# RWKV-6 with mixture-of-depths: another written order of the turns, and the shift issued by SP

## The chip, the cores and the metric

One core of a Trainium2 chip runs the whole kernel. The metric is the device time of one execution in microseconds (us). The kernel before took 281.06 us (median of three runs, 280.52 to 287.19); a further execution was profiled.

## The reference, cut to what matters

Inputs: r, k, v, w of shape (4 samples, 8 heads, 768 steps, 48), u (8, 48), and a router with two weight matrices.

```
for t in range(768):                     # per sample and head, state is 48 x 48
    y[t]  = r[t] @ (state + outer(u * k[t], v[t]))
    state = w[t][:, None] * state + outer(k[t], v[t])
x = y with heads side by side            # (4, 768, 384)
scores = x @ w_gate
for each sample: for the 128 rows with the highest score:
    out[row] = x[row] + sigmoid(score) * (relu(x[row] @ w1) @ w2)
all other rows: out[row] = x[row]
```

## The kernel before, in words

**Tiles.** A sample's 768 steps are cut into 6 chunks of 128, so there are 24 chunks, n = 0 to 23. A chunk of an input is a tile of 128 steps x 384 (8 heads x 48), 192 KB. Inside a chunk the recurrence is written as matmuls. The decay is taken in logarithms: `lnw` (ACT, line 136) takes ln w; `sums` (line 140) sums them along the steps with a triangular matmul (PE, L145) and ACT makes `fall` (L148) and `rise` (L159), the exponentials of the sum and of its negative. `e` is `fall` moved up by one step. For the first three chunks it is a second matmul and exponential (L154, L155); from then on it is the **shift**: two DMAs from SBUF to SBUF, one of 112 rows and one of 15, issued by ACT (L158). `line` (L165) writes one row of `fall` to DRAM, `whole` (L173) reads it back across the partitions as `all`, the chunk's whole decay.

`scaled` (DVE, L204) makes K = k * e and R = r * rise. `turned` (L215, L217) transposes both with eight PE transposes and copies them out of PSUM on ACT as Kt and Rt. `scores` (L235) multiplies them in quarters into a PSUM buffer P, of which there are two, used in turn (`p_bufs[n % 2]`); `fresh` (L251) puts the new state's products in the same buffer; `masked` (DVE, L263) makes `sc`; `states` makes s1 and mid (DVE, L276 to L281) and the next chunk's state s0 (POOL, L283). `from_state` (L294) and `from_chunk` (L312) add the two parts of the result into P. `own_products` (POOL, L180, L181), `own_sum` (DVE, L188) and `own_values` (POOL, L195) make the part with u. `result` (DVE, L334, L340) adds it to P, giving x, takes the router's score, and SP stores x (L344).

**The order is written by hand.** One loop runs over turns, n = -4 to 23. A turn does different stages of different chunks: `sums` of chunk n+4, `scaled` of n+3, `turned` of n+2, `scores` and `states` of n+1, the result of n. Every engine works through its own instructions in the written order, and so does the queue of SP, which issues all loads, stores, `line` and `whole`. At a turn's end `load` fetches w, k, r and v of chunk n+7. Each of the first seven turns also loads a piece of w1 or w2 (L537; three of 512 KB, four of 384 KB).

**The mixture.** When a sample's six chunks are done, `mixture` finds its 128 best rows and runs the two matmuls. It is a generator of 28 pieces, which the next sample's six turns take up, 4 or 5 a turn, half of them in the middle of the turn and the rest at its end: two `every` (PE L356, ACT L359), six `ahead` (DVE, L369), the rank (PE L378), pick, index and gather (DVE L393, PE L399, POOL L412), `xeT` (L420, L422), the gate, eight pieces of `ps_h` (L451, with `hid` on ACT, L456, after each four), and eight of `ps_f` (L461), the last with `ye` (DVE, L467) and a scatter (POOL, L470). All share one PSUM buffer, so `ps_e` of the second half waits until `every` of the first has been copied, and so on. The last sample's mixture runs alone at the end.

**A wait put in by hand.** `from_state` and `from_chunk` write other rows of the same PSUM bank, so `from_chunk` waits on an instruction of ACT that comes after `from_state`: the copy of Kt of the same turn (`after`, L219). Where none is named, ACT copies two columns of P first (`seen`, L308).

Of the kernel before, what the change touches and what calls it, by code (L numbers as in the profile page):

```python
# [17 lines left out]
L = 128  # L18
# [5 lines left out]
def _rows(ap, n):  # L24

    return dataclasses.replace(ap, ap=[[0, n]] + [list(x) for x in ap.ap])
# [10 lines left out]
def kernel(  # L37
# [14 lines left out]
    nc = tc.nc  # L52
# [6 lines left out]
    NCH = S // L  # L59
# [19 lines left out]
    chunks = [(b, ci) for b in range(B) for ci in range(NCH)]  # L79
# [14 lines left out]
    all_bufs = [consts.tile([L, HP], FP32, name=f"all_buf{i}") for i in range(6)]  # L94

    work = {n: {} for n in range(N)}

    def load(n, names="wkrv"):
        if n >= N:
            return  # L100
        b, ci = chunks[n]
        for name in names:
            x, bufs = dict(w=(w, 5), k=(k, 7), r=(r, 7), v=(v, 10))[name]
            t = lev.tile([L, H, D], FP32, tag=name, name=name, bufs=bufs)
            src = x[b, :, ci * L:(ci + 1) * L, :].rearrange("h t d -> t h d")
            nc.sync.dma_start(out=t, in_=src)  # L106
            work[n][name] = t
# [22 lines left out]


    def lnw(n):
        if n < N:
            t = work[n]
            t["lw"] = lev.tile([L, C], FP32, tag="lw", name="lw", bufs=2)
            nc.scalar.activation(  # L136
                out=t["lw"], in_=t.pop("w").rearrange("p h d -> p (h d)"), func=AF.Ln
            )

    def sums(n):  # L140
        if not 0 <= n < N:
            return
        t = work[n]
        ps = psR.tile([L, 512], FP32, tag="r", name="ps_x")
        nc.tensor.matmul(ps[:, 0:C], tri, t["lw"], start=True, stop=True)  # L145
        fall = t["fall"] = lev.tile([L, C], FP32, tag="fall", name="fall")
        rise = t["rise"] = lev.tile([L, C], FP32, tag="rise", name="rise")
        nc.scalar.activation(  # L148
            out=fall, in_=ps[:, 0:C], func=AF.Exp, accum_out=guard[:, n, 0:1]
        )  # L150
        e = t["e"] = e_bufs[n % len(e_bufs)]
        if n < EARLY:
            strict = psR.tile([L, 512], FP32, tag="r", name="ps_x")
            nc.tensor.matmul(strict[:, 0:C], tri_s, t["lw"], start=True, stop=True)  # L154
            nc.scalar.activation(out=e, in_=strict[:, 0:C], func=AF.Exp)  # L155
        else:
            for lo, hi in ((0, L - 16), (L - 16, L - 1)):
                nc.scalar.dma_start(out=e[lo:hi], in_=fall[lo + 1:hi + 1])  # L158
        nc.scalar.activation(  # L159
            out=rise, in_=ps[:, 0:C], func=AF.Exp, scale=-1.0, accum_out=guard[:, n, 1:2]  # L160
        )

    def line(n):
        if 0 <= n < N:
            nc.sync.dma_start(out=lines[n:n + 1], in_=work[n]["fall"][0:1])  # L165
# [24 lines left out]
    def own_values(n):  # L190
        if not 0 <= n < N:
            return
        t = work[n]
        t["vo"] = lev.tile([L, H, D], FP32, tag="vo", name="vo")
        nc.gpsimd.tensor_mul(t["vo"], t["v"], t.pop("own").to_broadcast([L, H, D]))  # L195
# [12 lines left out]
    def turned(n):  # L208
        if not 0 <= n < N:
            return  # L210
        t = work[n]
        for name in "KR":
            ps = psR.tile([L, HP, L], FP32, tag="r", name="ps_t")
            for j in range(HP):
                nc.tensor.transpose(ps[:, j, :], t[name][:, 2 * j:2 * j + 2, :], ident)  # L215
            t[name + "t"] = lev.tile([L, HP, L], FP32, tag=name + "t", name=name + "t", bufs=3)
            ins = nc.scalar.copy(out=t[name + "t"], in_=ps)  # L217
            if name == "K":
                after[n - 2] = ins  # L219
        t.pop("R")  # L220

    after = {}
    quarters = [(par, sub) for par in (0, 1) for sub in (0, 1)]

    def half(i, n=HB):
# [101 lines left out]
    def result(n):  # L327
        if not 0 <= n < N:
            return
        t = work.pop(n)  # L330
        b, ci = chunks[n]
        x = lev.tile([L, C], FP32, tag="x", name="x", bufs=3)
        pairs = dict(q=2, d=D)
        nc.vector.tensor_add(  # L334
            x.rearrange("p (j q d) -> p q j d", **pairs),
            t["P"][:, :, 0:YW].rearrange("p q (j d) -> p q j d", d=D),
            t["vo"].rearrange("p (j q) d -> p q j d", q=2),
        )
        scr = lev.tile([L, C], FP32, tag="scr", name="scr")
        nc.vector.tensor_tensor_reduce(  # L340
            out=scr, in0=x, in1=wg_bc, scale=1.0, scalar=0.0, op0=ALU.mult, op1=ALU.add,
            accum_out=score[:, b, ci:ci + 1],
        )
        nc.sync.dma_start(out=views[b][b, ci * L:(ci + 1) * L, :], in_=x)  # L344
# [132 lines left out]
    def run(*steps):  # L477
        for g in steps:
            yield from g
# [3 lines left out]
    def mix(n):  # L483
        for _ in range(n):
            next(mixing, None)
# [4 lines left out]
    with tc.manual_schedule():  # L490
        nc.scalar.preload_act_table_set("natural_log_exp_and_others")
        load(0, "wkr")
        load(1, "wkr")
        nc.sync.dma_start(out=u_bc, in_=_rows(u, L))
        load(0, "v")
        load(1, "v")
        load(2)
        nc.sync.dma_start(out=wg_bc, in_=_rows(moe_w_gate, L))
        load(3)

        nc.gpsimd.iota(row, pattern=[[1, L]], base=0, channel_multiplier=0)
        nc.gpsimd.iota(col, pattern=[[0, L]], base=0, channel_multiplier=1)
        nc.vector.tensor_tensor(out=tri, in0=col, in1=row, op=ALU.is_ge)
        for t in e_bufs:
            nc.gpsimd.memset(t[L - 32:L], 1.0)
        nc.vector.tensor_tensor(out=tri_s, in0=col, in1=row, op=ALU.is_gt)
        nc.vector.tensor_tensor(out=ident, in0=col, in1=row, op=ALU.is_equal)
        for t in k_bufs + r_bufs:
            nc.vector.memset(t[:, :, D:HB], 0.0)
        for t in all_bufs:  # L510
            nc.gpsimd.memset(t, 1.0)
        nc.vector.tensor_tensor(out=behind[:, 0:L], in0=col, in1=row, op=ALU.is_lt)
        for i in (0, 1):
            nc.vector.tensor_copy(out=mask[half(i)], in_=behind[half(i), half(i)])
            nc.vector.memset(p_bufs[i], 0.0)
        nc.vector.tensor_copy(out=slots, in_=row)
        nc.vector.memset(ones, 1.0)
        nc.vector.memset(ones_f, 1.0)
        nc.gpsimd.memset(behind[:, L:S], 1.0)
        nc.gpsimd.iota(count, pattern=[[-L, NCH]], base=S - 1, channel_multiplier=-1)  # L520
        nc.vector.tensor_copy(out=behind_n, in_=count)
        nc.gpsimd.iota(
            number[:, :, :, 0], pattern=[[S, B], [L, NCH]], base=0, channel_multiplier=0
        )
        nc.gpsimd.iota(
            number[:, :, :, 1], pattern=[[0, B], [0, NCH]], base=0, channel_multiplier=1
        )
        nc.vector.tensor_copy(out=ids, in_=number)

        lnw(0)  # L530
        for n in range(-4, N):
            if n >= 0 and chunks[n][1] == 0 and n > 0:
                mixing = run(mixing, mixture(chunks[n][0] - 1))
            k1 = per_turn[chunks[n][1]] if n >= NCH else 0
            if n >= 0 and n < len(weights):
                to, of = weights[n]
                nc.sync.dma_start(out=to, in_=of)  # L537
            whole(n + 3)
            lnw(n + 5)
            from_state(n)  # L540
            turned(n + 2)
            scores(n + 1)
            fresh(n + 1)
            own_values(n + 1)
            masked(n + 1)
            states(n + 1)
            mix(k1 // 2)
            from_chunk(n)
            result(n) if n >= 0 else None
            own_products(n + 3)  # L550
            own_sum(n + 2)
            sums(n + 4)
            line(n + 4)
            load(n + AHEAD)
            scaled(n + 3)
            mix(k1 - k1 // 2)
        mixing = run(mixing, mixture(B - 1))
        mix(1000)

        total = setup.tile([L, 1], FP32)  # L560
        nc.vector.tensor_reduce(out=total, in_=guard, axis=AX.XY, op=ALU.add)
        ps = psM.tile([L, C], FP32, tag="m", name="ps_w")
        nc.tensor.matmul(ps[0:1, 0:1], total, ones_f, start=True, stop=True)
        wide = setup.tile([1, 1], INT32)
        nc.vector.tensor_scalar(
            out=wide, in0=ps[0:1, 0:1], scalar1=LIMIT, scalar2=0.5, op0=ALU.is_le, op1=ALU.is_lt
        )
# [72 lines left out]
```

## Time and profile before

| what | before |
|---|---|
| median of three runs | 281.06 us (280.52 to 287.19) |
| the profiled execution | 279.03 us |
| its span, first to last instruction | 277.2 us |
| mean TensorE clock granted | 0.821 |
| PE matmul, weight load | 201.8 us (73%), 153.6 us (55%) |
| DVE, ACT, POOL busy | 141.2 (51%), 76.9 (28%), 96.8 us (35%) |
| DMA moved | 34.29 MB |
| 31 to 90 us: PE busy, clock, DMA | 48.80 us, 0.71, 185 GB/s |
| 90 to 224 us: PE busy, clock, DMA | 107.63 us, 0.89, 123 GB/s |
| 224 to 277 us: PE busy, clock, DMA | 30.95 us, 0.81, 25 GB/s |
| `masked` of chunks 0, 1, 8, 13, 23 begins | 28.1, 33.55, 90.56, 137.1, 227.9 us |

A profile line of a group names the code line, the engine, the operation and output<-inputs. PEld is the load of a matmul's fixed operand; SPq and ACTq are the sequencers that issue DMAs. In a line of the timeline, the brackets at the end hold how long the engine had been idle and what ended it. In the chain that ended last, each piece was released by the one before it, or by its engine's previous instruction. The clock is a share of full speed; it was 0.50 or 1.00 in every stretch of the trace.

### The profile page before, as it was taken

The numbers are of one execution on the slowest core, as the hardware profiler recorded it, in microseconds if no ns is written. First come the engines' busy times: TensorE is split into PE (matmuls) and PEld (weight loads), VectorE is DVE, ScalarE is ACT, GpSimd is POOL, SyncE is SP. The second block draws the span as 40 slices with busy tenths as digits, with TensorE's granted clock in tenths as the row PEclk, the third lists the DMA queues.
The fourth block names the chain that finished last, engine by engine and source line by source line (L and its number), as shares of the span: only waits on it lengthen the run. The fifth ranks groups of instructions, "written<-read, shape, count | busy, mean of one in ns | idle before, by whom it ended". The sixth has DMA issues, their size and how long they took to land.

```text
span 277.2 us, 8475 instructions
## 1 busy us (share of the span) xinstructions
PE 201.8 (73%) x3592; PEld 153.6 (55%) x3592; DVE 141.2 (51%) x330; ACT 76.9 (28%) x198; POOL 96.8 (35%) x119
## 2 busy tenths in 40 slices
PE   3336769877987568999875889998749799527750
PEld 1115556756665357766554767676538675317620
DVE  7210657551567938535689376346893641451010
ACT  3316333232333234233442241425312101100100
POOL 5400555046232565432554255235443410110010
PEclk9955975775579659999987699999876999955995
DMA  7899795879886878677776544672211000100010
GB/s 150 181 202 203 146 220 118 211 161 202 205 205 174 195 171 181 131 161 172 172 160 135 114 112 101 137 170 87 61 58 31 31 31 31 57 16 15 0 35 8
DMA packets 121508, 34.29 MB, mean 124 GB/s; under 512 B 113651, under 2 KB 120694, under 8 KB 121462
## 3 DMA queue, kind: packets, MB, share of 16 engines
q1 hardware_dynamic: 117632, 28.00, 47.0%
q10 hardware_dynamic: 3318, 4.10, 5.1%
q0 software_dynamic: 512, 1.57, 1.8%
q8 instruction: 30, 0.49, 0.8%
q14 instruction: 16, 0.13, 0.1%
HBM read 24.02 MB, written 5.54 MB: 107 GB/s over the span
## 4 chain that ended last, share of the span: by engine, by line
PE 35%; DVE 21%; issue 15%; DMA 12%; SPq 9%; ACT 4%; POOL 1%; ACTq 1%; DVEq 0%; POOLq 0%
PE ps_t L215 6%; SPq L106 6%; PE ps_h L451 6%; DMA w<-in_w_dram 5%; PE ps_p L312 5%; PE ps_p L235 4%; PE ps_f L461 4%; DVE r_buf L204 4%; DVE ahead L369 3%; PE ps_x L145 3%; DVE k_buf L204 3%; PE ps_p L251 3%; DVE x L334 2%; DMA e_buf<-fall 2%; DVE sc L263 2%
## 5 line engine op out<-in xcount | busy, mean ns | idle before, releaser
L263 DVE TENSOR_TENSOR sc<-ps_p,mask 128x512 f32<-128x512 f32 x24 | 16.6, 691 | 61.1 <-PE ps_p L251 61.1
L283 POOL TENSOR_TENSOR s<-mid,all_buf 128x192 f32<-128x192 f32 x20 | 11.7, 586 | 91.2 <-DVE mid L281 39.7
L312 PE MATMUL ps_p<-v,sc 64*64 64x48 f32 x768 | 32.2, 242 | 6.2 <-ACT Kt L217 6.2
L312 PEld LDWEIGHTS ps_p<-v,sc 64*64 64x64 f32 x768 | 29.3, 157 | 11.4 <-ACT Kt L217 6.8
L195 POOL TENSOR_TENSOR vo<-v,own 128x384 f32<-128x384 f32 x24 | 23.4, 974 | 21.7 <-DVE own L188 21.5
L451 PE MATMUL ps_h<-xeT,w 128*128 128x128 f32 x192 | 27.8, 299 | 3.4 <-ACT hid L456 2.8
L145 PE MATMUL ps_x<-lw,tri 128*128 128x384 f32 x48 | 27.0, 651 | 4.3 <-ACT lw L136 4.3
L334 DVE TENSOR_TENSOR x<-ps_p,vo 128x384 f32<-128x384 f32 x24 | 13.3, 556 | 31.8 <-PE ps_p L312 26.3
L451 PEld LDWEIGHTS ps_h<-xeT,w 128*128 128x128 f32 x192 | 25.3, 208 | 6.0 <-ACT hid L456 3.6
L181 POOL TENSOR_TENSOR rk<-rk,u_bc 128x384 f32<-128x384 f32 x24 | 25.6, 1065 | 5.6 <-DMA u_bc<-in_u_dram 3.8
L148 ACT ACTIVATE fall<-ps_x 128x384 f32<-128x384 f32 x24 | 11.8, 490 | 54.4 <-PE ps_x L145 54.4
L180 POOL TENSOR_TENSOR rk<-r,k 128x384 f32<-128x384 f32 x24 | 26.0, 1082 | 2.0 <-DMA r<-in_r_dram 2.0
L215 PE MATMUL ps_t<-ident,r_buf 128*128 128x128 f32 x96 | 19.7, 341 | 8.4 <-ACT e_buf L155 5.0
L461 PE MATMUL ps_f<-w,hid 128*128 128x384 f32 x64 | 23.7, 501 | 2.7 <-ACT hid L456 2.1
L215 PE MATMUL ps_t<-ident,k_buf 128*128 128x128 f32 x96 | 18.6, 326 | 9.3 <-DVE k_buf L204 9.3
L294 PEld LDWEIGHTS ps_p<-s,Rt 48*64 48x64 f32 x704 | 15.6, 157 | 11.8 <-issue 3.3
L204 DVE TENSOR_TENSOR r_buf<-r,rise 128x384 f32<-128x384 f32 x24 | 21.7, 905 | 0.0
L159 ACT ACTIVATE rise<-ps_x 128x384 f32<-128x384 f32 x24 | 11.8, 491 | 33.0 <-DVE k_buf L204 15.6
L235 PE MATMUL ps_p<-Rt,Kt 48*64 48x64 f32 x768 | 20.8, 262 | 0.0
L235 PEld LDWEIGHTS ps_p<-Rt,Kt 48*64 48x64 f32 x768 | 17.2, 168 | 5.5 <-issue 5.5
L215 PEld LDWEIGHTS ps_t<-ident,r_buf 128*128 128x128 f32 x96 | 13.5, 172 | 11.6 <-ACT e_buf L155 5.4
L294 PE MATMUL ps_p<-s,Rt 48*64 48x48 f32 x704 | 18.8, 246 | 0.6 <-DVE mid L281 0.6
(79 smaller groups left out, 267.8 us busy)
## 6 DMA issues: line engine op xcount, KB each, us to landing
w<-in_w_dram SPq DMA_DIRECT2D x25, 192.0 KB
k<-in_k_dram SPq DMA_DIRECT2D x25, 192.0 KB
r<-in_r_dram SPq DMA_DIRECT2D x25, 192.0 KB
v<-in_v_dram SPq DMA_DIRECT2D x25, 192.0 KB
out_dram<-x SPq DMA_DIRECT2D x24, 192.0 KB
e_buf<-fall ACTq DMA_DIRECT2D x21, 168.0 KB
w<-in_moe_w_dram SPq DMA_DIRECT2D x3, 512.0 KB
w<-in_moe_w_dram SPq DMA_DIRECT2D x4, 384.0 KB
```

The lines of the kernel that those rows point to most:

```text
L145: nc.tensor.matmul(ps[:, 0:C], tri, t["lw"], start=True, stop=True)
L180: nc.gpsimd.tensor_mul(rk, t["r"], t["k"])
L181: nc.gpsimd.tensor_mul(rk, rk, u_bc)
L195: nc.gpsimd.tensor_mul(t["vo"], t["v"], t.pop("own").to_broadcast([L, H, D]))
L204: nc.vector.tensor_mul(t[to][:, :, 0:D], t.pop(of), t.pop(by).rearrange("p (h d) -> p h d", d=D))
L215: nc.tensor.transpose(ps[:, j, :], t[name][:, 2 * j:2 * j + 2, :], ident)
L235: nc.tensor.matmul(P[half(sub), par, j * HB:(j + 1) * HB], t["Kt"][half(par, D), j, half(sub)], t["Rt"][half(par, D), j, half(sub)], start ...
L263: nc.vector.tensor_mul(t["sc"], t["P"][:, :, 0:SC].rearrange("p q (j t) -> p q j t", t=HB), _heads(mask, 2, HP),)
L294: nc.tensor.matmul(t["P"][half(sub), par, j * D:(j + 1) * D], t["Rt"][half(par, D), j, half(sub)], t["s1" if sub else "s0"][half(par, D), ...
L312: ins = nc.tensor.matmul(t["P"][half(sub), par, j * D:(j + 1) * D], t["sc"][half(sub), par, j, :], t["v"][half(sub), 2 * j + par, :], star ...
L451: nc.tensor.matmul(ps[:, q, :], w1[:, dc, (f0 + q) * L:(f0 + q + 1) * L], xeT[:, dc, :], start=(dc == 0), stop=(dc == NDC - 1),)
L461: nc.tensor.matmul(ps, hid[:, fc, :], w2[:, fc, :], start=(fc == 0), stop=(fc == NFC - 1))
```

## The change

It rewrites the turn and the loads ahead of it:

- The loop's body has another order. The loads of chunk n+7 come first in the turn instead of last, and are left out in the very first turn, where before they fetched chunk 3 a second time. `result` moves to the start of the next turn. `turned` stands ahead of `from_state`. `sums` moves from behind `from_chunk` to behind `from_state`, and `lnw` takes the logarithm of chunk n+4 in the turn that sums it, where before it took n+5. `own_products` and `own_values` come ahead of `scaled`. `scaled` and `own_sum` come ahead of `masked` and `states`.
- The half of the mixture's pieces that lay behind `states` now lies behind `line`, ahead of `scaled`.
- The shift is issued by SP instead of ACT.
- `from_chunk` of chunk n waits for `fall` of chunk n+4 instead of Kt of n+2.
- k, r and v have one buffer fewer each; the first loads have another order.

```diff
-            x, bufs = dict(w=(w, 5), k=(k, 7), r=(r, 7), v=(v, 10))[name]
+            x, bufs = dict(w=(w, 5), k=(k, 6), r=(r, 6), v=(v, 9))[name]
...
-        if n < N:
+        if 0 <= n < N:
             t = work[n]
             t["lw"] = lev.tile([L, C], FP32, tag="lw", name="lw", bufs=2)
...
-        nc.scalar.activation(
+        after[n - 4] = nc.scalar.activation(
             out=fall, in_=ps[:, 0:C], func=AF.Exp, accum_out=guard[:, n, 0:1]
         )
...
             for lo, hi in ((0, L - 16), (L - 16, L - 1)):
-                nc.scalar.dma_start(out=e[lo:hi], in_=fall[lo + 1:hi + 1])
+                nc.sync.dma_start(out=e[lo:hi], in_=fall[lo + 1:hi + 1])
...
-            ins = nc.scalar.copy(out=t[name + "t"], in_=ps)
-            if name == "K":
-                after[n - 2] = ins
+            nc.scalar.copy(out=t[name + "t"], in_=ps)
...
         load(0, "wkr")
         load(1, "wkr")
+        load(2, "w")
         nc.sync.dma_start(out=u_bc, in_=_rows(u, L))
         load(0, "v")
+        load(2, "kr")
+        load(3, "w")
+        nc.sync.dma_start(out=wg_bc, in_=_rows(moe_w_gate, L))
         load(1, "v")
-        load(2)
-        nc.sync.dma_start(out=wg_bc, in_=_rows(moe_w_gate, L))
-        load(3)
+        load(3, "kr")
+        load(2, "v")
+        load(3, "v")
...
-        lnw(0)
         for n in range(-4, N):
-            if n >= 0 and chunks[n][1] == 0 and n > 0:
-                mixing = run(mixing, mixture(chunks[n][0] - 1))
-            k1 = per_turn[chunks[n][1]] if n >= NCH else 0
+            if n > -4:
+                load(n + AHEAD)
             if n >= 0 and n < len(weights):
                 to, of = weights[n]
                 nc.sync.dma_start(out=to, in_=of)
             whole(n + 3)
-            lnw(n + 5)
+            result(n - 1)
+            if n > 0 and chunks[n][1] == 0:
+                mixing = run(mixing, mixture(chunks[n][0] - 1))
+            pieces = per_turn[chunks[n][1]] if n >= NCH else 0
+            lnw(n + 4)
+            turned(n + 2)
             from_state(n)
-            turned(n + 2)
+            own_products(n + 3)
+            own_values(n + 1)
+            sums(n + 4)
+            line(n + 4)
+            mix(pieces // 2)
+            scaled(n + 3)
+            own_sum(n + 2)
             scores(n + 1)
             fresh(n + 1)
-            own_values(n + 1)
             masked(n + 1)
             states(n + 1)
-            mix(k1 // 2)
             from_chunk(n)
-            result(n) if n >= 0 else None
-            own_products(n + 3)
-            own_sum(n + 2)
-            sums(n + 4)
-            line(n + 4)
-            load(n + AHEAD)
-            scaled(n + 3)
-            mix(k1 - k1 // 2)
+            mix(pieces - pieces // 2)
+        result(N - 1)
```

## The prediction, made before the change was run

> **What bounds the kernel now.** I read the page's slices first, then the chain that ended last, the waits (SP's own too) and the timeline of single turns. All times are us.
>
> The slices, each 6.93 us: PE busy, the TensorE clock granted, what the DMA engines moved.
>
> ```profile
> PE   3336769877987568999875889998749799527750
> PEclk9955975775579659999987699999876999955995
> GB/s 150 181 202 203 146 220 118 211 161 202 205 205 174 195 171 181 131 161 172 172 160 135 114 112 101 137 170 87 61 58 31 31 31 31 57 16 15 0 35 8
> ```
>
> Three stages: to about 90 the DMA moves 200 GB/s in its good slices while the clock is halved in many; from 90 to 224 PE is nearly full; after 224 the last sample's mixture runs alone. The chain in the first stage (start, length, what):
>
> ```profile
> 44.75 0.59 ACT fall L148 x2
> 45.36 2.37 DMA e_buf<-fall
> 47.75 0.37 SPq L106
> 48.17 4.42 DMA v<-in_v_dram
> 52.60 4.15 DMA w<-in_w_dram
> 57.21 0.58 ACT Kt L217
> 57.83 1.32 PE ps_p L312 x32
> ```
>
> Loads, not arithmetic, end these waits: SP holds a load back until the shift issued by ACT has landed, then lw waits for its w, and Kt and the PE products stand behind lw on ACT. The waits (us in total, times, longest) agree; the first two are SP's:
>
> ```profile
> SPq L344 <- DVE x L334: 66.2, 16, 9.3
> SPq L106 <- DMA e_buf<-fall: 17.2, 7, 3.7
> ```
>
> ```profile
> ACT lw L136 <- DMA w<-in_w_dram: 23.0, 8, 7.2
> ```
>
> In the middle the chain is PE after PE, one turn here:
>
> ```profile
> 115.47 0.84 PE ps_x L145 x2
> 116.31 1.34 PE ps_h L451 x12
> 117.65 0.61 PE ps_p L294 x32
> 118.26 1.16 PE ps_t L215 x8
> 119.41 0.62 PE ps_p L235 x32
> ...
> 121.29 0.61 ACT hid L456
> ...
> 122.85 1.06 PE ps_p L312 x32
> ```
>
> So a turn's own PE work at full clock is 0.84 + 0.61 + 1.16 + 0.62 + 0.54 (L251, timeline) + 1.06 = 4.8, and a mixture piece is 0.67. But each sample's first two turns hold PE up. The timeline there:
>
> ```profile
> 142.51 0.66 PE L215 MATMUL ps_t<-ident,k_buf 128*128 128x128 f32 x4 [1.36 <-DVE k_buf L204]
> 152.08 0.19 PE L378 MATMUL ps_r<-ones,ahead 128*128 128x1 bf16 x1 [2.97 <-DVE ahead L369]
> 153.54 0.32 PE L399 MATMUL ps_i<-ids,pick 128*128 128x2 bf16 x6 [1.28 <-DVE pick L393]
> ```
>
> **What the Trainium skill says.** "DMA: Bandwidth & Descriptors", section "Queues, rings and completion order": SP and ACT each own one ring per DMA engine, consumed in ring order, and an engine alternates between rings packet by packet. So ACT's shift passes waiting loads today (2.37 and 3.84 in the chain), and on SP it stands behind them. "TensorE: Matmul & The Clock Gate", section "What's actually happening": too little activity in a window of about 3.4 us halves the clock. The trace agrees: waits of 1.36 and 0.45 from 141 on precede a stretch with the clock at 0.50 (144.0 to 147.4 in the table by stretches), the 2.97 wait another (150.8 to 157.6); waits of 0.69 precede none.
>
> **The change, part by part.** My base is the profiled execution, 279.03 with a span of 277.2; the median of the runs is 281.06, 2.0 above it. I sum differences and take them from the median.
>
> *Loads.* Before, chunk 3 is loaded twice (each input shows x25 for 24 chunks): 4 x 192 KB. At 200 GB/s one load is 0.98, so 3.9 of DMA time goes. w(n+4) now has about three turns between issue and use instead of one, which should end most of lw's 23.0. One buffer fewer of k, r and v: a load at the start of turn n refills what turn n-2 used, nothing unless a turn runs late.
>
> *Shift on SP.* ACT loses two issues (about 1.45 a turn, 116.96 to 118.41 in the timeline); ACT is 28% busy, so nothing by itself. SP per turn: w, k, r, v 3.2, two lines 1.2, output 0.4, shift 1.4, line 0.25 = 6.5 of a turn of 8 or more; hidden in the middle. If turns fell below 6.5 SP would bind. A wait is added: SP stands at the output until x(n-1) is there, then at the shift until fall(n+4). Queued behind are the line and the next loads, which have turns to spare. scaled(n+4) a turn later is what needs the shift.
>
> *Early stage.* The first shift, chunk 3's, is now behind 28 loads and two broadcasts: 30 x 0.98 + start 1.5 + landing 2.4 = 33.3. DVE does scaled (0.6 + 0.9) and own (0.55) ahead of masked(1): 35.4, against 33.55 before. Then each turn carries 3.9 of loads, 1.3 to 2.6 of weights (384 KB at the 313 GB/s of the table by stretches at 61 to 63, up to 512 KB at 200), output, shift and small ones 1.7 to 1.9: 6.9 to 8.4. PE at half clock needs 9.6 a turn, at full clock 4.8. Before, these turns took 8.14 on average (33.55 to 90.56, seven). I take 7.7: masked(8) at 35.4 + 7 x 7.7 = 89.3, so -1.3. With 6.9 it is -6.9; with 8.9 it is +7.1.
>
> *A sample's first two turns, full clock, 0 = first transpose.* PE: transposes 1.16, from_state 1.77, sums 2.61, first ps_e 3.15. ACT must finish fall and rise ahead of every, so ps_e goes on at 4.2 (gap 1.05, before 0.57). Second ps_e 4.74, scores 5.36, fresh 5.9, from_chunk 6.96. DVE: masked, states to 7.35, three ahead 2.65: 10.0; only then result, so x frees the bank at 10.6. PE's second turn: sums done at 9.6, scores wait to 10.6 (gap 1.05), from_chunk ends 12.8. DVE: score 0.64, two ahead 1.3, scaled 1.3, own 0.54, masked 0.69, states 0.7, last ahead 0.4: 16.1; rank and ps_r 0.5; pick 0.96; ps_i 0.3: 18.0. Before, from_state to from_state over the same two turns was 133.9 to 153.8: 19.9. Gain 1.9: the 1.36 + 0.45 wait on scaled and its half-clock stretch go, two gaps near 1 come.
>
> *Other four turns.* Same work. The wait for hid grows from 0.69 to 0.9 (ACT has fall and rise in front) twice; the small waits on scaled (0.69, 0.44, 0.28) go, but the half clock after pick now lies on transposes. I call it zero.
>
> *Order on POOL, lnw, the manual wait.* POOL needs 1.08 + 1.07 + 0.97 + 0.59 = 3.7 a turn; hidden by PE's 4.8 or more. from_chunk now waits for fall(n+4), which ends under scores and fresh (1.2); without that cover it costs 0.5 a turn.
>
> *End.* result(23) comes after the last ye (0.62), so x and score (1.15) lie ahead of the last mixture's ps_e: +1.2.
>
> Sum: early -1.3, first sample's pair -1.0 (partly inside the early stage), two more -3.8, end +1.2 = -4.9. 281.06 - 4.9 = 276.2.
>
> **Rivals.**
> 1. *As summed*: 276, own range 272 to 280. Chance 0.44.
> 2. *The early stage runs at the DMA's rate* (6.9 a turn): PE would have to stay at full clock although idle 2 us a turn, against which the clock row speaks; the removed duplicate and ring order speak for it. -4.9 - 5.6: 270.6. Chance 0.20.
> 3. *The shift's new place is hidden by nothing early*: turns of 8.9, since scaled stands on DVE ahead of masked and states. -4.9 + 8.4: 284.6. For it: 2.4 to 3.8 of landing becomes a queue of a turn's loads. Against: a whole turn of slack. Chance 0.20.
> 4. *Slower, by the clock*: each sample has four PE waits of 0.9 to 1.05 (ps_e, scores, hid twice) in its six turns, twelve in all. If one tips the clock, at least 3.4 us run at half, 1.7 lost. The 4.9 gained plus the 5.6 that are 2% make 10.5, so it decides from seven of the twelve on; with eight, 281.06 - 4.9 + 13.6 = 289.8. For it: 1.36 + 0.45 did so. Against: 1.23 at 82.5 did not. Chance 0.16.
>
> That the change does nothing at all is the edge of 1 and 3.
>
> **How the numbers follow.** About 2% is what a measurement of this kernel tells from no change: 275.4 and 286.7. Faster: most of rival 2 (0.19) and just under half of 1 (0.21): 0.40. Slower: 4 (0.16) and a tail of 3 (0.03): 0.19. Same: 0.41. The range, 268 to 288, takes in 2 and 3 and leaves out half of 4 and the edges of 2 and 3.
>
> **What would show it.** Right: inputs x24; masked(1) near 35 and masked(8) near 89; lw no longer waiting for w; SP's wait on fall in front of the shift; k_buf waits of PE gone in the middle and waits on every and x near 1 in their place; pairs of 18. Wrong: masked(8) after 95 or before 85; PE clock in the middle below 0.9 outside the pairs; scaled waiting on the shift in the middle turns.

## The result, and the profile after

The kernel after took 270.23 us (median of four runs, 266.93 to 271.71); the kernel before 284.12 (four runs, 280.52 to 288.25). Executions of one kernel differ by 1 to 3% among themselves; the ratio, taken from the fast ones of each, is 0.957, with a 95% interval of 0.945 to 0.969: faster. The profiled execution took 270.15 with a span of 268.2, against 279.03 and 277.2: 9.0 less. All times are us.

In the new file `scaled` is L205, the shift L159, `load` L107, `scores` L233, `result` L332, `every` L357, `ahead` L367, the rank L376, pick L391, `hid` L454. The slices of the kernel after, each 6.7 us (PE busy, clock, DMA):

```profile
PE   3728557859958859889986698899746988824880
PEclk9995956795696866999997679999995799955995
GB/s 146 196 200 200 142 168 229 199 199 240 210 155 199 200 147 166 178 149 139 119 196 151 172 107 144 139 32 91 32 61 62 32 18 46 12 47 33 0 0 42
```

The three stages are still there. I compare by the start of each turn's first PE instruction, since `masked`, my marker in the prediction, lies some 3 later in its turn now. A sample's first two turns, while `mixture` works on its rank and its gather, I call a pair:

| from, to | before | after | difference |
|---|---|---|---|
| start to turn 6 | 79.08 | 77.13 | -1.95 |
| turns 6, 7 (first pair) | 19.97 | 20.12 | +0.15 |
| turns 8 to 11 | 34.88 | 35.07 | +0.19 |
| turns 12, 13 (second pair) | 19.86 | 17.90 | -1.96 |
| turns 14 to 17 | 34.83 | 34.10 | -0.73 |
| turns 18, 19 (third pair) | 19.94 | 17.90 | -2.04 |
| turns 20 to 22 | 24.85 | 25.53 | +0.68 |
| turn 23 to the last mixture's `ps_e` | 5.44 | 5.44 | 0 |
| `ps_e` to the end of the last `ye` | 28.64 | 27.80 | -0.84 |
| what follows it | 9.7 | 7.2 | -2.5 |

The chain of the kernel after in the first stage (start, length, what):

```profile
36.59 0.73 SPq L107
37.38 0.91 SPq L537
39.32 0.57 SPq L159
39.93 4.15 DMA e_buf<-fall
44.11 0.56 DVE k_buf L205
```

Before, the chain went through the shift on ACT, the landing of v and of w, and Kt. Now it is SP's own issuing, then the shift's landing, then `scaled`. In the view of waits (whole run; us in total, times, longest) DVE's largest row says the same; two rows of SP's own follow:

```profile
DVE k_buf L205 <- DMA e_buf<-fall: 33.4, 7, 8.8
```

```profile
SPq L342 <- DVE x L332: 36.9, 8, 8.1
SPq L159 <- ACT rise L160: 15.8, 8, 4.4
```

`lw` waits for w once, 1.6 (eight times, 23.0, before). SP's wait at the output fell from 66.2 to 36.9, but all of it lies in later stages: before turn 8, SP waited there for x 0.4 in the kernel before and not at all in the kernel after, and SP's waits at the shift (L159) lie behind turn 8 too. What is new in the first stage is DVE's 33.4 of waiting for the shift, at `scaled`, all before turn 8. In the chain the shift of chunk 4 leaves SP at 39.32, though ACT had its `fall` ready at 29.8: SP was still issuing the turn ahead. In the middle, the waits of the second pair on PE's timeline:

```profile
136.31 0.54 PE L354 MATMUL ps_e<-ident,score 128*128 128x128 f32 x3 [1.18 <-ACT every L357]
143.16 1.08 PE L233 MATMUL ps_p<-Rt,Kt 48*64 48x64 f32 x32 [1.91 <-DVE x L332]
148.39 0.18 PE L376 MATMUL ps_r<-ones,ahead 128*128 128x1 bf16 x1 [1.20 <-DVE ahead L367]
150.04 0.31 PE L397 MATMUL ps_i<-ids,pick 128*128 128x2 bf16 x6 [1.48 <-DVE pick L391]
```

Before, this row of waits was 1.36 on `k_buf` (and 0.45 on `r_buf`), 2.97 on `ahead`, 1.28 on pick. The 2.97 became 1.20 here and 2.62 in the third pair, which was no longer for it. What the four have in common is that DVE ends all but the first, and the table by stretches over the second and third pairs shows why they are shorter. The first columns are start:end, us, PE busy, PEld busy, and then DVE busy; PE's clock is the third number from the end. Before, then after:

```profile
133.93:153.79 19.86, 12.92 (x294) 10.24 (x293) 16.36 (x37) 7.13 (x19) 8.51 (x9) 0.84 0.78 174
188.62:208.56 19.94, 13.00 (x294) 10.26 (x294) 16.35 (x37) 6.36 (x17) 8.50 (x9) 0.84 0.22 62
```

```profile
132.32:150.22 17.90, 12.13 (x295) 10.03 (x293) 16.89 (x34) 5.93 (x16) 9.97 (x9) 0.90 0.79 172
184.32:202.22 17.90, 10.71 (x294) 8.64 (x293) 16.89 (x34) 5.52 (x15) 9.97 (x9) 0.97 0.21 57
```

A pair belongs to DVE, nearly. It does 16.4 to 16.9 of work in it; before, 3.5 of idle time came on top (19.86 - 16.36), now 1.0. PE's clock didn't count: the two pairs after took 17.90 each, with the clock at 0.90 and 0.97 and PE's busy time 1.4 apart (and e8's took 17.99 and 17.90 at 0.82 and 0.83).

The exception is the start. Until the pair's first `masked`, 5.58 in, DVE has to wait for PE, which waits for `every` on ACT; from there to the second `masked`, 8.8 later, DVE stands idle for 0.07 in all. The first `masked` on DVE's timeline, in the kernel after and in e4 below:

```profile
137.90 0.69 DVE L261 TENSOR_TENSOR sc<-ps_p,mask 128x512 f32<-128x512 f32 x1 [0.25 <-PE ps_p L249]
```

```profile
138.85 0.69 DVE L261 TENSOR_TENSOR sc<-ps_p,mask 128x512 f32<-128x512 f32 x1 [1.52 <-PE ps_p L249]
```

Both stand 5.6 behind the start of their pair, though DVE had more to do ahead of it in the first. So work of DVE that stands ahead of the first `masked` costs nothing as long as it fits into that time, and work behind it costs its full length. Before, DVE waited 1.34 at the first `masked` and then again, 1.31 at x.

### The profile page after: what moved, and what is told of

Same layout as the page of the kernel before. It is cut to its first block, busy times and chain, and to the rows that moved or that the text cites. A ratio compares the mean times of both kernels' runs of the same rounds, so it can differ in the third digit from the quotient of the medians.

```text
span 268.2 us, 8468 instructions
## 1 busy us (share of the span) xinstructions
PE 198.0 (74%) x3592; PEld 154.3 (58%) x3592; DVE 142.7 (53%) x330; ACT 74.5 (28%) x200; POOL 101.2 (38%) x119
## 4 chain that ended last, share of the span: by engine, by line
PE 42%; DVE 17%; SPq 13%; DMA 12%; issue 7%; ACT 5%; POOL 0%; DVEq 0%; POOLq 0%; ACTq 0%
PE ps_f L459 9%; SPq L107 9%; PE ps_h L449 8%; DMA e_buf<-fall 7%; DVE ahead L367 5%; PE ps_p L310 5%; PE ps_t L216 4%; PE ps_x L146 4%; PE ps_p L233 4%; PE ps_p L292 4%; DMA xe<-out_dram,idx 2%; DVE sc L261 2%; PE ps_p L249 2%; SPq L174 2%; ACT rise L160 2%
## 5 line engine op out<-in xcount | busy, mean ns | idle before, releaser
L205 DVE TENSOR_TENSOR k_buf<-k,e_buf 128x384 f32<-128x384 f32 x24 | 20.8, 868 | 43.6 <-DMA e_buf<-fall 33.4
L218 ACT COPY Kt<-ps_t 128x512 f32<-128x512 f32 x24 | 14.1, 586 | 95.8 <-PE ps_t L216 95.8
L310 PE MATMUL ps_p<-v,sc 64*64 64x48 f32 x768 | 32.9, 240 | 2.7 <-issue 2.5
L261 DVE TENSOR_TENSOR sc<-ps_p,mask 128x512 f32<-128x512 f32 x24 | 16.4, 685 | 32.0 <-PE ps_p L249 32.0
L310 PEld LDWEIGHTS ps_p<-v,sc 64*64 64x64 f32 x768 | 30.4, 157 | 3.8 <-issue 3.4
L146 PE MATMUL ps_x<-lw,tri 128*128 128x384 f32 x48 | 27.9, 670 | 5.7 <-ACT lw L137 5.7
L181 POOL TENSOR_TENSOR rk<-r,k 128x384 f32<-128x384 f32 x24 | 28.6, 1193 | 6.4 <-DVE own L189 4.3
L182 POOL TENSOR_TENSOR rk<-rk,u_bc 128x384 f32<-128x384 f32 x24 | 26.3, 1095 | 6.2 <-DMA u_bc<-in_u_dram 4.4
L233 PEld LDWEIGHTS ps_p<-Rt,Kt 48*64 48x64 f32 x768 | 16.8, 165 | 16.5 <-issue 9.1
L196 POOL TENSOR_TENSOR vo<-v,own 128x384 f32<-128x384 f32 x24 | 24.4, 1015 | 4.4 <-DVE x L332 4.4
L233 PE MATMUL ps_p<-Rt,Kt 48*64 48x64 f32 x768 | 20.6, 259 | 4.0 <-DVE x L332 4.0
L367 DVE SCALAR_TENSOR_TENSOR ahead<-every,score,behind 128x768 bf16<-128x768 f32 (+5 forms) x24 | 19.8, 868 | 1.2 <-ACT every L357 1.2
L205 DVE TENSOR_TENSOR r_buf<-r,rise 128x384 f32<-128x384 f32 x24 | 18.8, 783 | 0.0
```

The costliest lines, as they stand in the source:

```text
L181: nc.gpsimd.tensor_mul(rk, t["r"], t["k"])
L182: nc.gpsimd.tensor_mul(rk, rk, u_bc)
L205: nc.vector.tensor_mul(t[to][:, :, 0:D], t.pop(of), t.pop(by).rearrange("p (h d) -> p h d", d=D))
L233: nc.tensor.matmul(P[half(sub), par, j * HB:(j + 1) * HB], t["Kt"][half(par, D), j, half(sub)], t["Rt"][half(par, D), j, half(sub)], start ...
L310: ins = nc.tensor.matmul(t["P"][half(sub), par, j * D:(j + 1) * D], t["sc"][half(sub), par, j, :], t["v"][half(sub), 2 * j + par, :], star ...
L367: nc.vector.scalar_tensor_tensor(out=ahead[:, c, lo:S], in0=every[:, lo:S], scalar=score[:, b, c:c + 1], in1=behind[:, 0:S - lo], op0=ALU. ...
```

## The experiments

My theory: the gain is the pairs', from DVE's order; the shift's new place costs time in the first stage, where SP is busy, and pays for it in the middle, where ACT's issues would stand in front of `hid` and `every`. The rivals: the gain is the removed duplicate load; or the shift on SP is the gain by itself. Not tested apart are the buffers taken from k, r and v, the order of the first loads, and the new wait of `from_chunk`.

**e1: the kernel after once more.**

> The changed kernel once more, for the spread of its trace. If the gain lies in the order, the second and third samples' first two turns take 17.9 us again (19.9 before) and turn 23 starts 5 to 6 us earlier than before. If the 2.5 us at the program's end (6.8 us after the last products instead of 9.3) belong to the change, the end takes 6.8 us again; if they are chance, it takes anything from 6.8 to 9.3. Time 270.

271.66 (267.38 to 271.93), with the kernel before at 286.89 on this chip (seven runs, 280.19 to 332.56). The later pairs were 18.0 and 17.9 again, and turn 23 starts 5.0 earlier than before. What follows the last `ye` took 7.2 again.

**e2: the kernel after, shift issued by ACT as before.**

```diff
-                nc.sync.dma_start(out=e[lo:hi], in_=fall[lo + 1:hi + 1])
+                nc.scalar.dma_start(out=e[lo:hi], in_=fall[lo + 1:hi + 1])
```

> The changed kernel with the shift issued by ACT again. Theory (the gain is the order, and the shift on SP costs in the early stage because it stands behind the loads): scaled no longer waits for the shift, chunk 1 is masked before 35 us instead of 36.9, turn 6 starts 1 to 3 us earlier, the middle is unchanged: 267 to 270. Rival (taking the two issues off ACT is what pays): the middle gets slower by over 0.3 us a turn, 275 or more. Rival (the end of the program follows the instruction count of SP's queue): the last 6.8 us become about 9.

278.83 (275.1 to 282.0; the kernel after 266.93 to 271.71). The theory held for the first stage, but its unchanged middle and its 267 to 270 did not: the middle is the first rival's. Turn 8 starts at 88.74 instead of 97.25, and turns 8 to 17 take 98.3 instead of 87.1. So the shift's new place costs 8.5 early and returns 11.2 in the ten turns that follow. The second half is on PE's and then on ACT's timeline of this kernel:

```profile
104.44 0.94 PE L449 MATMUL ps_h<-xeT,w 128*128 128x128 f32 x6 [2.57 <-ACT hid L454]
115.99 1.46 PE L459 MATMUL ps_f<-w,hid 128*128 128x384 f32 x2 [2.63 <-ACT hid L454]
```

```profile
101.85 1.42 ACTq L159 DMA_DIRECT2D e_buf<-fall  x2
103.32 0.49 ACT L160 ACTIVATE rise<-ps_x 128x384 f32<-128x384 f32 x1 [1.49 <-DVE r_buf L205]
103.71 0.20 ACT L160 ACTIVATION_READ_ACCUMULATOR rise<-ps_x 128x1 f32 x1
103.80 0.59 ACT L454 ACTIVATE hid<-ps_h 128x512 f32<-128x512 f32 x1
```

The two issues take ACT 1.42; `rise` and `hid` are behind them, and PE waits 2.57 instead of the 0.96 of the kernel after. `every` does the same (2.8 instead of 1.18), and the pair pays for it. It took 19.57 and 19.54, with the same DVE work as in the kernel after (16.91); the first `masked` stands 7.24 behind the pair's start instead of 5.58, 1.66 later, which is what the wait on `every` grew by:

```profile
134.99 0.54 PE L354 MATMUL ps_e<-ident,score 128*128 128x128 f32 x3 [2.84 <-ACT every L357]
```

```profile
136.58 0.69 DVE L261 TENSOR_TENSOR sc<-ps_p,mask 128x512 f32<-128x512 f32 x1 [1.91 <-PE ps_p L249]
```

So the new order alone doesn't shorten the pairs by much: it needs the shift's issues out of the way of `every`. The old order had `sums` and the shift behind the mixture's pieces; PE waited 0.69 for `hid` there.

**e3: the kernel before, chunk 3 loaded once.**

```diff
-            load(n + AHEAD)
+            if n > -4:
+                load(n + AHEAD)
```

> The kernel before, with chunk 3 loaded once. Theory (order): the 0.79 MB saved are 3.9 us of transfers in the early stage, but half of them are given back to PE at half clock: 278 to 280, and the first two turns of the later samples still take 19.9 us. Rival (the double load is the bulk of the gain): 271 to 274.

279.04 (273.91 to 280.31). Turn 6 starts 4.5 earlier (74.58), but turn 9 at 108.44 against 108.75: the lead was gone after the first sample's gather, whose read took 5.22 here, with the clock at half from 93.6 to 107.3. The later pairs took 20.3 and 20.6, so the duplicate is not where the pairs' gain comes from. Nor does the trace show a gain at turn 23, which starts at 234.12 (233.41 before). What it is worth to the total can't be told: the median is inside my range, but the kernel before took 280.19 or more on this chip and as little as 277.98 on another.

**e4: the kernel after, with the result of n at the end of turn n.**

```diff
-            result(n - 1)
...
             from_chunk(n)
+            result(n)
             mix(pieces - pieces // 2)
-        result(N - 1)
```

> The changed kernel with result(n) at the end of turn n, after from_chunk and ahead of the second half of the mixture's pieces. Theory (in the changed kernel PE's scores wait 1.9 us for x, which stands behind three ahead on DVE): this wait goes, the pairs of turns take about 16.5 us instead of 17.9, 265 to 267. Rival (the pair is bound by DVE's own sum, so that the wait only moves to ps_r): pairs stay at 17.9, 270.

276.14 (275.28 to 277.26): my theory fell. The 1.91 on x went, but the pair took 19.1 instead of 17.9, and the wait came back at the rank:

```profile
150.71 0.19 PE L376 MATMUL ps_r<-ones,ahead 128*128 128x1 bf16 x1 [3.69 <-DVE ahead L367]
```

The second turn's x and score (1.1) lie on DVE ahead of pick again, while ahead of the first `masked` DVE waits 1.52. The late `result` is no cost with a wait of 1.91 beside it; it is part of the gain, because it takes one result out of DVE's gapless stretch and puts it where DVE waits for PE. The third pair shows it once more: 19.09 again, with 1.5 less of DVE work (15.25), all of it ahead of the first `masked`, where the wait is 3.29 instead. A wait of PE is no price as long as DVE has work until PE is back. The pairs account for 2.4 of the 6 by which this kernel is slower; the rest is spread over the other stretches.

**e5: the kernel after, shift by ACT for the chunks below 10 only, from then on by SP.**

```diff
-                nc.sync.dma_start(out=e[lo:hi], in_=fall[lo + 1:hi + 1])
+                (nc.scalar if n < 10 else nc.sync).dma_start(
+                    out=e[lo:hi], in_=fall[lo + 1:hi + 1])
```

> The changed kernel with ACT issuing the shift of chunks 3 to 9, which lie in turns without mixture, and SP the others. Theory (behind the loads on SP the shift costs the early stage 8 us, and ACT's two issues cost the mixing turns because hid and every stand behind them): turn 8 starts near 89 as with all shifts on ACT (97.3 changed), turns 8 to 23 take 130 to 132 as in the changed kernel (145 with all on ACT): 260 to 264. Rival (the early lead only empties the loads' lead, and the middle pays it back whoever issues the shift): turn 18 at 184 or later, 269 to 272.

264.14 (263.56 to 264.9), before at 284.15 (seven runs): ratio 0.946, interval 0.938 to 0.954. Turn 8 starts at 91.17 and turns 8 to 17 take 87.1: most of e2's early gain and all of the new kernel's middle. That confirms both halves of e2; the pairs are back at 18.05 and 17.91.

**e6: the kernel before, with only the shift moved to SP.**

> The kernel before with the shift on SP and nothing else. Theory (the two edits need each other: in the old order hid and every come ahead of the shift's issues on ACT, so moving the shift frees nothing, and the early stage pays for the place behind the loads): 280 to 288, the middle as before, 8.7 us a turn. Rival (the move to SP alone brings the gain): 271 to 274.

288.34 (281.0 to 292.97), before at 284.15 (277.98 to 285.24), and the lowest are 3 apart the same way: the move alone is no gain. Its profiled execution is its slowest run, 292.97, so I read no stages from it.

**e7: the kernel after, shift by ACT again, but written behind `rise` and behind the first half of the mixture's pieces.**

```diff
+    def shift(n):
+        if EARLY <= n < N:
+            t = work[n]
+            for lo, hi in ((0, L - 16), (L - 16, L - 1)):
+                nc.scalar.dma_start(out=t["e"][lo:hi], in_=t["fall"][lo + 1:hi + 1])
...
             mix(pieces // 2)
+            shift(n + 4)
             scaled(n + 3)
```

> The changed kernel with ACT issuing all shifts again, but behind rise and behind the mixture's pieces in the middle of the turn. Theory (what costs with ACT is that hid and every stand behind the two issues): PE's waits for hid fall from 2.6 to about 0.9 and for every from 4 to about 1.2, early stage fast, turn 8 near 89: 261 to 265. Rival (it is the issues' time on ACT, or the loads' lead running out, wherever they stand): 272 or more.

261.31 (259.93 to 264.89): ratio 0.934, interval 0.921 to 0.947, the best version of this study; it beats both kernels. Turn 8 starts at 87.95. On ACT's timeline the same two issues now let `rise` and `hid` by, and PE's wait on `hid` is 0.96 again:

```profile
100.33 0.20 ACT L157 ACTIVATION_READ_ACCUMULATOR rise<-ps_x 128x1 f32 x1
100.42 0.60 ACT L457 ACTIVATE hid<-ps_h 128x512 f32<-128x512 f32 x1
100.73 0.83 ACTq L165 DMA_DIRECT2D e_buf<-fall  x1
```

So neither queue is right or wrong in itself: what counts is what stands ahead of the issue and behind it. The Trainium skill ("DMA: Bandwidth & Descriptors", section "Issuing engines are not separate DMA queues") says that spreading issues over engines only saves the sequencer's time to issue, which is usually small next to the transfer. Here that time was what mattered in the middle (1.42 on ACT), and the place in the queue early. The pairs took 17.96 and 17.94. Turns 8 to 17 also took 84.0 instead of 87.1; PE's waits are about the same and its busy time is 3.7 less (clock 0.92 against 0.89). Why the clock was higher I can't say.

**e8: the kernel after, chunk 3 loaded twice** (e3's edit undone in the new order).

> The changed kernel with chunk 3 loaded a second time in the first turn, as before. Theory (with the shift behind the loads the early stage follows the transfers, so 3.9 us more of them show in full up to turn 8 and stay, since the middle has no slack to give back): turn 8 at 101, 273 to 275. Rival (given back in the middle, as removing them was in the old order): 270 to 272.

272.58 (271.54 to 273.9), between the two forecasts. By the stages the theory holds: turn 8 starts at 100.40, 3.2 later than in the kernel after, and what follows takes the same. All of the 3.2 is there at the start of turn 0 (28.52 against 25.28). The duplicate is worth 2 to 3 in the new order, where its four issues and 4 x 192 KB stand in front of the first shift.

**e9: the kernel before, with `result` a turn later and nothing else.**

```diff
             whole(n + 3)
+            result(n - 1)
...
             from_chunk(n)
-            result(n) if n >= 0 else None
...
+        result(N - 1)
```

(The start of a sample's mixture moves behind it.)

> The old order with one step of the new one: result(n) at the start of turn n+1, ahead of its other work, instead of behind from_chunk. Theory (the gain of a sample's first two turns comes from result standing a turn later, so that it no longer lies on DVE ahead of scaled and the ahead of the same turn): the wait of 1.36 + 0.45 on scaled shrinks by about the 1.15 of result, the 2.97 on ahead shrinks too, each pair takes about 18.5 instead of 19.9, and the span is about 4 below the old one: 272 to 275 in the profiled execution, the early stage within 2 of the old one. Rival (the gain comes from scaled standing ahead of masked and states): pairs stay within 0.5 of 19.9, time within 2 of the kernel before.

270.72 (267.2 to 274.21), before at 281.89 on this chip: ratio 0.962, interval 0.950 to 0.975. The pairs are 18.48 each, as the theory had it. What it had not: turn 8 starts at 92.32, 6.7 earlier. SP's wait at the output is 32.0 instead of 66.2 over the whole run:

```profile
SPq L344 <- DVE x L334: 32.0, 6, 9.1
```

That isn't the cause: before turn 8 SP waits there for x 0.4 or less in both kernels. In that stage SP's waits for the shift to land fell from 13.1 to 8.1, the DMA moved 198 GB/s instead of 169 from 29 to 61, and PE's clock was 0.84 and 0.79 in its two halves instead of 0.75 and 0.68. Which of these came first stays open.

From turn 8 to turn 23 the kernel takes 135.4, before 134.4 and after 130.5: in the turns outside the pairs it loses what the pairs gain. So this one step equals the whole change in time, but not by the same way.

**e10: the kernel after, with `scaled` and `own_sum` back behind `states`.**

```diff
             mix(pieces // 2)
-            scaled(n + 3)
-            own_sum(n + 2)
...
             states(n + 1)
+            own_sum(n + 2)
+            scaled(n + 3)
             from_chunk(n)
```

> The new kernel with scaled and own_sum put back behind states, so that a late shift on SP no longer holds up masked and states of the same turn, and PE's next transposes have from_chunk alone to hide scaled. Theory (the early stage pays for the shift's queueing because scaled stands in front on DVE; in the middle, scaled's early place only removes the waits on k_buf): turn 8 starts 2 to 6 earlier than 97.25, the waits of PE on k_buf come back in the middle (0.4 to 1.4 a turn in a sample's first two turns, 0.7 elsewhere), turn 8 to turn 18 takes 88 to 92 instead of 87.1, time 266 to 273. Rival (the place of scaled is what gives the pairs their 2): pairs back at 19.9 and turn 8 no earlier, time 275 or more.

285.36 (284.27 to 285.47): ratio 1.018, interval 1.010 to 1.025. The rival is right on all counts: the pairs are back at 19.8, and turn 8 starts at 104.52, 7.3 later. The table by stretches has a pair, and then turns 0 to 3 and 4 to 7:

```profile
140.91:160.71 19.80, 13.82 (x294) 10.65 (x294) 15.54 (x35) 6.04 (x16) 8.51 (x9) 0.83 0.69 151
...
27.42:63.59 36.17, 28.24 (x536) 21.22 (x537) 17.87 (x34) 10.55 (x28) 16.30 (x18) 0.67 0.84 188
63.59:104.52 40.93, 32.68 (x554) 24.64 (x554) 25.32 (x51) 11.41 (x30) 15.32 (x15) 0.60 0.77 181
```

DVE has less work in this pair than in the kernel after (15.54 against 16.89), but 4.3 of idle time, 3.7 of it at the first `masked`, which stands 5.64 behind the start as ever: DVE waits for PE's products where it could have done `scaled`, and does `scaled` in the stretch behind. In the first stage PE's transposes, first in the turn, wait for `scaled` every turn, and the clock is 0.67 and 0.60 there:

```profile
54.31 0.63 PE L216 MATMUL ps_t<-ident,k_buf 128*128 128x128 f32 x4 [1.43 <-DVE k_buf L205]
```

I had taken `scaled` in front of `masked` for the cost of the first stage. With it behind, the wait on the shift nearly vanishes from DVE's timeline (0.32 where it shows) and the turns get longer (9.0 on average from turn 1 to turn 6), with PE's waits for `scaled` and more half clock (0.78 and 0.74 in the kernel after). Which of the two costs more is not shown.

The pairs of all orders together, as DVE work + DVE idle time:

| kernel | result | scaled | work | idle | pair |
|---|---|---|---|---|---|
| before | same turn | end of turn | 16.36 | 3.50 | 19.86 |
| e9 | next turn | end of turn | 16.07 | 2.41 | 18.48 |
| e10 | next turn | behind `states` | 15.54 | 4.26 | 19.80 |
| e4 | same turn | ahead of `masked` | 16.73 | 2.36 | 19.09 |
| e4, third pair | same turn | ahead of `masked` | 15.25 | 3.84 | 19.09 |
| e2 (shift on ACT) | next turn | ahead of `masked` | 16.91 | 2.66 | 19.57 |
| after | next turn | ahead of `masked` | 16.89 | 1.01 | 17.90 |

Both steps are needed for the 17.9, and each acts by what DVE does while PE is at work. With them, the shift's issues must not stand in front of `every`.

## Why the prediction was right, and where it was not

The predicted 276 is 5.8 above the median, inside the range. Faster, which is what came, had a chance of 0.40, the same time 0.41. By its own terms, the sum is -4.9 against -9.0 of span:

**Two more pairs, -1.9 each: right.** 18.0 predicted, 17.90 and 17.90 measured. The walk along PE's and DVE's order was the right tool. Its details were less good: the waits on `every` and x were to be 1.05 each and are 1.18 and 1.91. The second changes nothing, since DVE works on meanwhile (e4 took the 1.91 away, and the pair got longer). The first is on the path, and 1.66 more of it cost 1.66 (e2).

**First stage -1.3, first sample's pair -1.0: together right to 0.5 (-2.3 predicted, -1.8 at turn 8), but by errors that cancelled.** The first shift was to land at 33.3 and landed at 35.5. After that I had the shift hidden by a whole turn of slack. It was not: SP was late from the first loads on, so that DVE waited 33.4 for the shift, of which only the first wait (8.8) was foreseen. SP's waits for x and `fall`, which were to hold the shift back, came only behind turn 8, and of the 66.2 that I read as a sign of a stage bound by loads, 60.8 lie between turn 8 and turn 23. "6.5 of a turn of 8 or more; hidden in the middle" held in the middle; in the first stage, two shifts left SP 7.8 apart (39.32 and 47.12), 6.0 of it issuing, and SP's queue with the landing behind it set the turn.

From turn 1 to turn 6 a turn took 8.2 on average (36.24 to 77.13) where I took 7.7, so `masked` of chunk 1 came at 36.94 instead of 35.4 and that of chunk 8 at 93.76 instead of 89.3. That the stage gained all the same is luck in the marker: `masked` lies some 3 later in its turn now, and I had counted that against the stage as if it were time lost. By the turns, turn 1 starts 1.05 later than before (36.24 against 35.19) and the next five take 8.2 each instead of 8.8. The earlier start of turn 0 (25.28 against 29.51) is used up by that turn's own wait for the first shift. The first pair gained nothing (20.12). Its first `scaled` still waited 2.99 for the shift, but with the shift on ACT again this pair was no shorter (23.1 in e2, 21.7 in e7), so what holds it is not shown. Without the shift's wait the stage would have gained some 9 more (e2, e7).

**"ACT is 28% busy, so nothing by itself": right for the old order, where the move alone gave nothing (e6), but the reason was wrong.** A share of busy time says nothing on what stands behind an issue. With the new order the issues on ACT cost 11.2 over ten turns (e2), unless they are written behind `rise` and `hid` (e7). The move to SP was a repair that the new order needed, and a dear one.

**Other four turns, 0: right in sum** (+0.19, -0.73, +0.68). The wait on `hid` was to be 0.9 and is 0.96. One of the signs of being wrong did show: the clock outside the pairs was 0.88 in turns 8 to 11 (0.94 before) and 0.90 in turns 14 to 17 (0.95 before). The turns took the same time.

**The end, +1.2: wrong, 0.** The last mixture's first `ps_e` comes 5.44 after turn 23 in both kernels. The first half of its rows needs the scores of the chunks before the last; the score of 23 is first needed in the second half, so x and score of 23 are hidden.

**Not in the sum:** -0.84 in the last mixture (less of `ps_h` at half clock) and -2.5 behind the last `ye`. The latter was 7.2 in e1 and e2, 8.3 in e4 and 9.9 in e7, kernels with the same instructions there, and 7.8 in e3, which ends as the kernel before does, so I don't put it down to the change. The differences of the terms are +0.5 - 0.2 + 0.1 - 1.2 - 0.8 - 2.5 = -4.1; the rest of the 5.8, about 2, is the gap between the median and the profiled execution that I had taken over from the kernel before and that the kernel after doesn't show.

**The rivals.** The second (first stage at the DMA's rate) did not come. The third had the mechanism, the shift's place hidden by nothing early, and was wrong on the price (8.9 a turn, 8.2 measured). The fourth, the clock, needed seven of twelve waits to tip it: in turns 9 to 19, neither of the two waits on `every` nor any of the four on `hid` came before a stretch at half clock, and of the two on x one did. Waits of 0.96 and 1.18 stood in stretches with the clock at 1.00.

## What to carry over

In a stretch where one engine's work nearly fills the time, here DVE with 16.4 of 19.9, an order gains what it takes off that engine's idle time, and a new wait on another engine costs only what reaches that engine: nothing for the 1.91 on x, all of the 1.66 more on `every`. So list where that engine is idle, and for whom it waits there, before pricing any wait. Before a DMA issue is moved to another queue, list what stands behind it on either queue, stage by stage; the third way, the same queue a few instructions later, can beat both (e7, 261.3 against 270.2). And test the parts one by one even where the whole won: here one step alone (e9) equalled it, and one part cost 9.

## What was not expected of the hardware

The same wait doesn't always move the clock. PE waited 1.91 for x before `scores` in two pairs, with the same work around it; the table by stretches has the clock after each:

```profile
143.00:147.00 4.00, 3.85 (x115) 3.76 (x115) 3.97 (x11) 0.00 (x0) 1.58 (x2) 0.57 0.53 129
...
195.00:199.00 4.00, 2.61 (x116) 2.47 (x116) 3.96 (x11) 0.00 (x0) 1.58 (x2) 1.00 0.32 102
```

0.57 the first time, 1.00 the second, and both pairs took 17.90. Nor is DVE's time for one instruction fixed. In the second pair of the kernel after, the product into `k_buf` on DVE's timeline, and POOL's timeline at the first of the two:

```profile
134.13 1.79 DVE L205 TENSOR_TENSOR k_buf<-k,e_buf 128x384 f32<-128x384 f32 x1
...
145.33 0.55 DVE L205 TENSOR_TENSOR k_buf<-k,e_buf 128x384 f32<-128x384 f32 x1
```

```profile
134.48 1.01 POOL L181 TENSOR_TENSOR rk<-r,k 128x384 f32<-128x384 f32 x1
135.57 1.20 POOL L182 TENSOR_TENSOR rk<-rk,u_bc 128x384 f32<-128x384 f32 x1
```

POOL did nothing from 144.6 to 148.2. The Trainium skill ("GPSIMD Engine Reference", section "1. Specifications") says that POOL shares its SBUF interfaces with VectorE and contends with DVE instructions that have two SBUF inputs, as this one has. The trace agrees, 1.79 beside POOL against 0.55 alone. So do the traces of all the kernels here: the two products of `scaled` took 0.54 to 0.58 each of the 287 times that no product of POOL ran beside them, and 0.86 to 1.98 the 88 times that both of the products above did. No run moved POOL's work to test it. So an order that fills DVE's idle time can come with longer work: 16.89 in a pair after, 15.54 in e10. Where DVE would have waited anyway, as in e4's two pairs with 16.73 and 15.25, that costs nothing.
